# The start-up of a fused attention and feed-forward kernel: an order of work written out for all five engines

## The chip, the core and the metric

The kernel runs on one core of a Trainium2 chip. A core has five engines with a queue each, which work through their instructions in order and wait for one another by semaphores: TensorE (PE in the profile, with its weight loads as PEld), VectorE (DVE), ScalarE (ACT), GpSimd (POOL) and SyncE (SP), which here issues all transfers between the chip's memory and the core. The metric is the device time of one execution in microseconds; the median of three runs is given.

## The reference

Attention without a triangle: for 8 batches of 8 heads with 576 positions of 64 numbers, a softmax of each query over its 64 numbers, a softmax of the keys over the positions, one 64 x 64 matrix per head, and its product with the queries. The result is the input of a gated feed-forward layer of 4608 tokens:

```python
q_s = np.exp(q - np.max(q, axis=-1, keepdims=True))
q_s = q_s / (np.sum(q_s, axis=-1, keepdims=True) + 1e-09)
k_s = np.exp(k - np.max(k, axis=2, keepdims=True))
k_s = k_s / (np.sum(k_s, axis=2, keepdims=True) + 1e-09)
kv = np.einsum('bhsd,bhse->bhde', k_s, v)
attn = np.einsum('bhsd,bhde->bhse', q_s, kv)
x = attn.transpose(0, 2, 1, 3).reshape(4608, 512)
out = ((x @ w_a) * (x @ w_b)) @ w_out     # w_a, w_b: 512 x 1536; w_out: 1536 x 512
```

The three weight matrices arrive as 64-bit floating point numbers, the rest as 32-bit ones.

## The kernel before

The 4608 tokens are worked on in nine chunks of 512. For a chunk the attention makes `xf`, four tiles of 128 x 512 (one for each pair of heads); the feed-forward layer goes over d_ff in 12 blocks of 128 (`NF`, the index `f`).

*Chunk 0* is also where the weights are converted. For each half block, ACT makes two parts of the 64-bit numbers (L103, L104: `wy` and `wr`), DVE shifts (L107), GpSimd adds (L110), DVE joins them (L113), ACT rounds to the TensorE's short form (`ws`, a cast, L79 or L941), and DVE subtracts to get the rest (L82 or L946). The finished block goes to a DRAM copy (`dw`) that the later chunks read. With it TensorE does the gate of the block: 24 products of 128 x 512 (`pt`, L537), 12 for `w_a`, whose result ACT copies to `ga` (L544), and 12 for `w_b`, with which DVE multiplies `ga` (L548). `project_first` (`po`, L572) takes `ga` times the block of `w_out` in full 32-bit numbers, four products, each of two passes. In between stand the attention tasks of chunk 1, one with each block from f = 3 on: a key task has an exponential (`kv_exp_t`), transposes into `pka` and `pkb` with copies back to `kt` (L299 to L301) and a product `pk` (L314); a query task has a reduction, eight exponentials of `qt` (L385, L388), a multiply (L394), transposes into `pq` (L468) and a product `px`. A late key task has a maximum (`m`), a transpose `pm`, a reduction `mc` and a diagonal tile `m` (L263, L265), and a product `pmx` (L271).

*Chunks 1 to 8* use seven products in place of eight for the two gates of a pair of blocks (i = 0 to 5): `kx`, `ky`, `ka` and `kp` of 12 matmuls each (L562), on sums of x (`xo`, L503 to L526) and of weights (in chunk 1 made by GpSimd from `dy`, `ws_y`, and split by ACT and DVE). Their combination `cc` is split into `gh` and `gl`, and `project` (L583) multiplies these with the split `wo`. The tasks of the next chunk's attention are dealt out between the products by `attend`.

*What sets the order.* The program is traced in an order, and a scheduler that has a timing model of the engines decides each engine's final list within the dependences; `tc.issue_after(x)` keeps what it holds from going ahead of x, and a dependence of the class NoSync orders two instructions of one engine without a semaphore. Before the change, the first part of chunk 0 is a string of steps written by hand (L991 to L999: `mc0`, `qs0` ... `G2`, each a method of `Startup` and its numbers). `in_order` (L1010) then ties SP's instructions of that part into one chain, and likewise those of ACT, DVE and GpSimd; after the f loop it ties TensorE's from `by_hand` on. In the f loop the conversion of block f + 1 is held behind the end of gate f - 2 (L1035), the exponentials of a task behind the last step of the start and a gate's end (L1048), the first half's `ga` behind the copies of a task (L1060 to L1063). The rest is the scheduler's choice.

## Time and profile before

| | us |
|---|---|
| median of three runs | 964.56 (964.27 to 965.41) |
| profiled execution | 966.23 |
| its span | 964.4 |
| busy in the span: TensorE, DVE, ACT, GpSimd | 932.9, 624.6, 391.5, 105.5 |
| TensorE clock granted, mean over the span | 0.998 |

The slices of the page show where the engines are full:

```profile
PE   5899999899999999999999999999999999999998
DVE  7987878886686747665566657566666547553433
ACT  7787744452372416322443244223622263221111
```

Each of the 40 slices is 24.1 us, and a digit is the busy share in tenths, 9 being 90% or more. The first slice is the start, which waits for loads; chunk 0 goes on to about 150 us, so it fills the first six slices, and chunk 1 lies in the next four. The list of times an engine waited names what it wanted to write, then the engine, tile and line that it lacked; "longest" is the longest single wait. The time of a program part in the trace is from the start of the span.

### The profile page before, as it was taken

The page shows a single profiled execution, that of the slowest core. Times are in us where ns is not written, and L with a number is a line of the kernel's source. Part 1 is how long each engine was busy: PE and PEld are TensorE (multiplying, and loading weights), DVE is VectorE, ACT ScalarE, POOL GpSimd, SP SyncE. Part 2 cuts the span into 40 slices and gives each one's busy share as a digit, 9 for nine tenths or more (in the row PEclk, how much of TensorE's full clock was granted, in tenths as well). Part 3 has the DMA queues.
Part 4 walks back from the last instruction along what each step waited for, and adds up shares of the span by engine and source line. Part 5 has one row for each costly group of instructions (what it writes and reads, how often), then busy time and mean ns, then how long its engine had stood idle before and what let it go on. Part 6 is the DMA issues. An engine that isn't in the chain of part 4 may idle for free.

```text
span 964.4 us, 17587 instructions
## 1 busy us (share of the span) xinstructions
PE 932.9 (97%) x6479; PEld 828.2 (86%) x6479; DVE 624.6 (65%) x1209; ACT 391.5 (41%) x1085; POOL 105.5 (11%) x88
## 2 busy tenths in 40 slices
PE   5899999899999999999999999999999999999998
PEld 3656656889999999989999999999999999999997
DVE  7987878886686747665566657566666547553433
ACT  7787744452372416322443244223622263221111
POOL 1544342422000000000000000000000000000000
PEclk9999999999999999999999999999999999999999
DMA  9999686989998968897799779877987689667761
GB/s 348 412 381 390 214 274 214 407 276 332 323 357 297 359 238 273 305 368 256 258 330 356 268 244 351 316 280 258 344 304 286 240 289 305 243 236 266 258 211 56
DMA packets 97588, 282.64 MB, mean 293 GB/s; under 512 B 11680, under 2 KB 12256, under 8 KB 97504
## 3 DMA queue, kind: packets, MB, share of 16 engines
q1 hardware_dynamic: 97504, 281.52, 81.6%
q8 instruction: 52, 0.85, 0.3%
q14 instruction: 32, 0.26, 0.1%
HBM read 241.40 MB, written 37.98 MB: 290 GB/s over the span
## 4 chain that ended last, share of the span: by engine, by line
PE 79%; DVE 7%; DMA 5%; issue 4%; POOL 2%; ACT 2%; SPq 1%; DVEq 0%; POOLq 0%
PE po L583 27%; PE kp L562 13%; PE ka L562 13%; PE kx L562 13%; PE ky L562 7%; POOL wr L110 2%; PE px L493 2%; PE pk L314 2%; DMA ws<-dw 1%; DMA raw<-in_w_ab 1%; DVE wy L113 1%; PE pt L537 1%; DMA ws_y<-dy 1%; SPq L448 1%; DMA kt_first<-in_kt 1%
## 5 line engine op out<-in xcount | busy, mean ns | idle before, releaser
L583 PE MATMUL po<-wo_w,gh 128*128 128x512 f32 x768 | 226.3, 395 | 1.0 <-ACT gh L79 1.0
L562 PE MATMUL kx<-xo,ws 128*128 128x256 f32 x1152 | 162.7, 283 | 0.0
L583 PEld LDWEIGHTS po<-wo_w,gh 128*128 128x128 f32 x768 | 138.6, 188 | 27.6 <-ACT gh L79 1.5
L562 PE MATMUL ka<-xo,ws 128*128 128x256 f32 x1152 | 160.9, 282 | 0.4 <-DVE cc L1147 0.4
L562 PE MATMUL kp<-xo,ws 128*128 128x256 f32 x1152 | 157.6, 283 | 1.5 <-DVE u L1120 1.5
L562 PEld LDWEIGHTS ka<-xo,ws 128*128 128x128 f32 x1152 | 149.5, 188 | 4.7 <-DVE cc L1147 0.6
L562 PEld LDWEIGHTS kp<-xo,ws 128*128 128x128 f32 x1152 | 147.7, 188 | 5.2 <-issue 1.6
L562 PEld LDWEIGHTS kx<-xo,ws 128*128 128x128 f32 x1152 | 149.5, 188 | 2.5
L583 PE MATMUL po<-wo_w,gl 128*128 128x512 f32 x384 | 136.4, 396 | 0.0
L79 ACT CAST gh<-cc 128x512 fp32r<-128x512 f32 x96 | 56.6, 620 | 134.5 <-DVE cc L1144 128.2
L1143 DVE TENSOR_TENSOR cc<-kp,u 128x512 f32<-128x512 f32 x48 | 33.1, 689 | 99.1 <-PE kp L562 98.9
L1134 ACT COPY cc<-kx 128x256 f32<-128x256 f32 x48 | 17.8, 371 | 182.9 <-PE kx L562 182.8
L583 PEld LDWEIGHTS po<-wo_w,gl 128*128 128x128 f32 x384 | 71.2, 188 | 16.0 <-DVE gl L82 0.4
L407 ACT ACTIVATE qt<-qt,st 128x64 f32<-128x64 f32 x224 | 75.0, 339 | 22.4 <-DVE st L404 17.2
L1133 DVE TENSOR_TENSOR cc<-kp,u 128x512 f32<-128x512 f32 x48 | 33.1, 689 | 76.1 <-PE kp L562 75.9
L562 PE MATMUL ky<-xo,ws 128*128 128x256 f32 x576 | 77.6, 284 | 3.2 <-DMA ws<-dw 2.2
L562 PEld LDWEIGHTS ky<-xo,ws 128*128 128x128 f32 x576 | 71.9, 188 | 4.5 <-DVE gl L82 2.1
L82 DVE TENSOR_TENSOR gl<-cc,gh 128x512 fp32r<-128x512 f32 x96 | 64.6, 692 | 10.6 <-ACT gh L79 10.6
L537 PE MATMUL pt<-xo,ws 128*128 128x512 f32 x288 | 70.2, 399 | 1.1 <-DVE ws L946 1.1
L244 POOL PARTITION_ALL_REDUCE mx<-m x20 | 18.3, 915 | 446.5 <-DVE m L255 446.5
L537 PEld LDWEIGHTS pt<-xo,ws 128*128 128x128 f32 x288 | 53.5, 189 | 14.0 <-DVE ws L946 1.6
L1119 ACT COPY u<-kx 128x512 f32<-128x512 f32 x48 | 28.0, 584 | 84.6 <-PE kx L562 84.3
(147 smaller groups left out, 1155.6 us busy)
## 6 DMA issues: line engine op xcount, KB each, us to landing
ws<-dw SPq DMA_DIRECT2D x312, 512.0 KB, 5.5
dw<-ws SPq DMA_DIRECT2D x42, 512.0 KB, 7.2
mr<-dq SPq DMA_DIRECT2D x112, 128.0 KB, 4.6
raw<-in_w_ab SPq DMA_DIRECT2D x24, 512.0 KB, 8.0
out<-ot SPq DMA_DIRECT2D x36, 256.0 KB, 4.7
vt<-in_v SPq DMA_DIRECT2D x28, 325.0 KB, 6.9
qt<-in_q SPq DMA_DIRECT2D x32, 256.0 KB, 5.5
kt<-in_k SPq DMA_DIRECT2D x24, 320.0 KB, 5.1
```

Of the source, the lines that this page charges most:

```text
L79: nc.scalar.copy(out=hi, in_=src)
L82: return nc.vector.tensor_tensor(out=lo, in0=src, in1=hi.bitcast(F32), op=ALU.subtract)
L110: nc.gpsimd.tensor_tensor(out=r, in0=u, in1=r, op=ALU.add)
L314: nc.tensor.matmul(pk[h * D:(h + 1) * D], kt[:, j, h], vt[:, j, h], start=(j == 0), stop=(j == J - 1),)
L407: nc.scalar.activation(out=qt[:, j, h], in_=qt[:, j, h], func=AF.Exp, bias=st[:, h, 0, j:j + 1], accum_out=st[:, h, 1, j:j + 1],)
L493: nc.tensor.matmul(px[:, s], w, m[:, s], start=(i == 0), stop=(i == 2))
L537: nc.tensor.matmul(pt, w[:, wp], x[g][:, xp], start=(g == 0 and i == 0), stop=(g == NP - 1 and i == 2),)
L562: ins = nc.tensor.matmul(pt[:, n], w[:, n, wp, c], x[:, xp, c], start=(first and n == 0 and i == 0), stop=(i == 5), skip_group_check=True,)
L583: ins = nc.tensor.matmul(po[t], a[:, ts], wo[f][:, w], start=(f == 0 and i == 0), stop=(f == NF - 1 and i == 2),)
L1119: nc.scalar.copy(out=u2, in_=kx)
L1133: nc.vector.tensor_tensor(out=cc[:, 3], in0=kp, in1=u3, op=ALU.add)
L1143: nc.vector.tensor_tensor(out=cc[:, 1], in0=kp, in1=u2, op=ALU.add)
```

## The change

The scheduler's freedom in the first part of the program is replaced by a table. Each piece of the program from the first load to the start of chunk 2 gets a name: the steps of the start keep theirs, and in the f loop and in chunks 1 and 2 a context manager `named` notes the instructions that each engine receives under `gate.f`, `proj.f`, `out.f`, `a.f`, `b.f` (conversion of w_out and of the two halves), `soft.n`, `turn.n`, `prod.n` (a task's exponentials, transposes with copies, and product), `split.m`, `w<op>.n`, `pair.n`, `attend.n`, `x.1`, `raw.f`, `load.n`, `sums.n`. `ORDER` has a string of these names for each engine; `name*k` takes the next k instructions of a piece, `name:j` the one at place j of those still left. `arrange` puts the instructions into that order with NoSync dependences, and every later instruction of the engine behind the last of the list. The `issue_after` holds of the f loop and the `in_order` chains go, but for SP's first loads; in chunk 1 `attend` holds nothing back. The computation is the same, instruction for instruction.

```diff
+ORDER = {
+    "PE": (
+        "tr1*4 tr0*5 tr1 pk0*10 pk1*10 pq0*4 tr2*5 pq1*4 px0 tr3:4 tr3*4 pq2*4 pk2*10 pk3*10 px1 "
...
+    ),
+    "DVE": (
...
 
+    def named(name):
+        before = traced[-1]
+        yield
+        start = next(n for n in reversed(range(len(traced))) if traced[n] is before) + 1
+        for ins in traced[start:]:
+            work.setdefault((ins.engine, name), []).append(ins)
...
-        getattr(Startup, name)(*(int(n) for n in step[len(name):]))
+        with named(step):
+            getattr(Startup, name)(*(int(n) for n in step[len(name):]))
...
-    in_order((E.SP,), loads, by_hand)
-    in_order((E.Activation, E.DVE, E.Pool), by_hand, len(traced))
-    startup = [at["last", 0].ins, at["last", 1].ins]
+    def behind_each_other(instructions):
+        for ins, before in zip(instructions[1:], instructions):
+            tc.add_manual_dep(
+                ins, before.name,
+                mybir.DependencyInfo(mybir.DependencyClass.NoSync, mybir.DependencyReason.DATA),
+                reason="in order",
+            )
+    def arrange(engine, names):
+        left = {name: list(found) for (of, name), found in work.items() if of == engine}
+        chain = []
+        for item in names.split():
+            name, _, count = item.partition("*")
+            name, _, place = name.partition(":")
+            for _ in range(int(count or 1)):
+                chain.append(left[name].pop(int(place or 0)))
+        behind_each_other(chain)
+        placed = {ins.name for ins in chain}
+        for ins in traced[by_hand:]:
+            if ins.engine == engine and ins.name not in placed:
+                behind_each_other([chain[-1], ins])
+    behind_each_other([ins for ins in traced[loads:by_hand] if ins.engine == E.SP])
...
-        with tc.issue_after(at["end", f - 2].ins):
+        with named(f"out.{f}"):
             convert_wo(f)
...
-            with tc.issue_after(startup[0]), tc.issue_after(at["end", max(f - 2, 1)].ins):
+            with named(f"soft.{n + 1}"):
                 tasks[n + 1][1]()
...
-                    with ExitStack() as pinned:
-                        for copy in copies or ():
-                            pinned.enter_context(tc.issue_after(copy.ins))
                         at["ga", f] = gate_half(f, pts[0])
...
-    in_order((E.PE,), by_hand, len(traced))
...
+            def multiply(pt, op, xop, first):
+                w = operand(op)
+                with part("pair"):
+                    return product(pt, w, x[xop], first)
...
-                attend(last)
+                with part("attend"):
+                    attend(c > 1 and last)
...
+    for engine, names in ORDER.items():
+        arrange(getattr(E, engine), names)
```

What the table does is seen in the engines' lists. No engine has an instruction more or less. SP's list differs in one swapped pair (the load of a weight block and that of a query tile, late in chunk 1), GpSimd's in neighbours that change places, by three places at most. The lists of TensorE, DVE and ACT differ up to about 245 us of the old trace.

The first place is ACT's list ahead of the copy `kt_116<-pka_611`, the copy of the first key task's transposes. The names are tiles; a number tells two tiles of one name apart. `wy` and `wr` are the parts of a half block, `qt_569` and `qt_787` query tiles. Before:

```order
L79 CAST ws_590<-wy_583 128x2x256
L103 ACTIVATE wy_681<-wo4_raw_527 128x512
L104 ACTIVATE wr_682<-wo4_raw_527 128x512
L103 ACTIVATE wy_690<-raw_571 128x512
L104 ACTIVATE wr_691<-raw_571 128x512
L388 ACTIVATE qt_569,qst2_727<-qt_569,qst_725 128x64 x7
L79 CAST ws_604<-wy_597 128x2x256
L300 COPY kt_116<-pka_611 128x512
```

After it the copy stands in these rows:

```order
L416 ACTIVATE kt_116<-kt_116,mc_562 128x640
L226 ACTIVATE wy_583<-raw_523 128x512
L511 ACTIVATE qt_787,qst2_935<-qt_787,qst_933 128x64
L227 ACTIVATE wr_584<-raw_523 128x512
L423 COPY kt_116<-pka_611 128x512
L511 ACTIVATE qt_569,qst2_727<-qt_569,qst_725 128x64 x2
L511 ACTIVATE qt_787,qst2_935<-qt_787,qst_933 128x64
L667 COPY ga_520<-pt0_486 128x512
```

The copy has moved from row 74 to row 66 of ACT's list (like rows counted as one), ahead of the conversion of `wy_597`, `wo4_raw` and `raw_571`, and the exponentials, a block of seven before, are dealt out singly, those of two query tiles by turns.

The second place is TensorE's list around the same task: the transposes `pka_611` and `pkb_612` and the product `pk_652` that needs the copies. Before:

```order
L572 MATMUL po3_515<-yo1_370,ga_482 128x512
L299 MATMUL pka_611<-ident_66,kt_116 128x128 x4
L299 MATMUL pkb_612<-ident_66,kt_116 128x128
L537 MATMUL pt0_623<-xo_284,ws_543 128x512 x3
L537 MATMUL pt0_623<-xo_316,ws_543 128x512 x3
L537 MATMUL pt0_623<-xo_403,ws_555 128x512 x3
L537 MATMUL pt0_623<-xo_424,ws_555 128x512 x3
L537 MATMUL pt1_624<-xo_284,ws_543 128x512 x3
L537 MATMUL pt1_624<-xo_316,ws_543 128x512 x3
L537 MATMUL pt1_624<-xo_403,ws_555 128x512 x3
L537 MATMUL pt1_624<-xo_424,ws_555 128x512 x3
L314 MATMUL pk_652<-vt_118,kt_116 64x65 x10
```

After, with `pt0_486` and `pt1_487` the gate of f = 2 and `pt0_623` that of f = 3:

```order
L695 MATMUL po0_512<-yo1_370,ga_482 128x512
L660 MATMUL pt1_487<-xo_424,ws_474 128x512 x3
L422 MATMUL pkb_612<-ident_66,kt_116 128x128
L695 MATMUL po1_513<-yo1_370,ga_482 128x512
L695 MATMUL po2_514<-yo1_370,ga_482 128x512
L660 MATMUL pt0_623<-xo_284,ws_543 128x512 x3
L695 MATMUL po3_515<-yo1_370,ga_482 128x512
L660 MATMUL pt1_624<-xo_284,ws_543 128x512 x3
L695 MATMUL po3_515<-yo_529,ga_520 128x512
L422 MATMUL pka_716<-ident_66,kt_126 128x128 x4
L695 MATMUL po0_512<-yo_529,ga_520 128x512
L437 MATMUL pk_652<-vt_118,kt_116 64x65 x10
```

The four transposes into `pka_611` now stand three rows ahead of these, in the middle of the gate before. Between them and the product of their task are pieces of two gates and of two projections, and the next key task's transposes (`pka_716`) come ahead of that product.

The third place is DVE's list at the start of chunk 1. `xo` are the operands of chunk 1's products, `wo` the split output weights, `mc_1429` and `m1_1431` the reduction and the diagonal tile of the late key task. Before:

```order
L82 TENSOR_TENSOR xo_1398<-xt_1396,xo_1398 128x512
L521 TENSOR_TENSOR xt_1390<-xf_113,xt_1390 128x512
L82 TENSOR_TENSOR xo_1401<-xt_1389,xo_1401 128x512
L82 TENSOR_TENSOR wo9_w_1218<-wo9_w_1218 128x512
L263 TENSOR_REDUCE mc_1429<-pm_1427 128x1
L82 TENSOR_TENSOR xo_1404<-xf_113,xo_1404 128x512
L82 TENSOR_TENSOR xo_1407<-xf_113,xo_1407 128x512
L82 TENSOR_TENSOR xo_1411<-xt_1390,xo_1411 128x512
L265 TENSOR_SCALAR m1_1431<-ident_66,mc_1429 128x128
L82 TENSOR_TENSOR ws_1527<-ws_y_1439,ws_1527 128x2x256
```

After:

```order
L205 TENSOR_TENSOR ws_1322<-wy_1315,ws_1322 128x2x256
L634 TENSOR_TENSOR xt_1390<-xf_113,xt_1389 128x512
L386 TENSOR_REDUCE mc_1429<-pm_1427 128x1
L388 TENSOR_SCALAR m1_1431<-ident_66,mc_1429 128x128
L639 TENSOR_TENSOR xt_1396<-xf_113 128x512
L527 TENSOR_REDUCE st_1580<-qt_1581 128x2x4
L671 TENSOR_TENSOR ga_1367<-pt1_1354,ga_1367 128x512
L527 TENSOR_REDUCE st_1580<-qt_1643 128x2x4
L205 TENSOR_TENSOR xo_1393<-xt_1390,xo_1393 128x512
L205 TENSOR_TENSOR ws_1527<-ws_y_1439,ws_1527 128x2x256
```

The reduction and the diagonal tile stand next to each other, ahead of the splits of `xo_1393`, `xo_1398`, `xo_1401`, `xo_1404`, `xo_1407` and `xo_1411`; two reductions of the attention of chunk 2 (`st_1580`) have come in between, and the split of `wo9` has gone to a place much later in chunk 1.

## The prediction

> **What bounds the kernel now.** I read first where TensorE stands still, stage by stage, then what it waits for there, and last the engine that made it wait. The first view gives seven stretches of the span (964.4 us): bounds, length, then busy us and instructions of TensorE, its weight loads, DVE, ACT and POOL, the granted clock, the DMA share and GB/s:

> ```profile
> 0.00:26.90 26.90, 14.66 (x116) 10.46 (x116) 19.96 (x43) 21.51 (x60) 5.91 (x12) 1.00 0.94 354
> 26.90:60.00 33.10, 31.96 (x127) 22.29 (x124) 32.74 (x50) 24.44 (x48) 15.74 (x12) 1.00 1.02 403
> 60.00:70.00 10.00, 7.68 (x39) 3.87 (x38) 8.43 (x16) 9.15 (x25) 5.00 (x4) 0.83 0.99 365
> 70.00:150.00 80.00, 76.32 (x342) 51.54 (x341) 60.58 (x100) 51.97 (x125) 34.51 (x26) 1.00 0.78 284
> 150.00:200.00 50.00, 44.07 (x306) 36.77 (x305) 40.13 (x84) 27.38 (x95) 17.53 (x13) 1.00 0.88 329
> 200.00:300.00 100.00, 100.00 (x768) 92.94 (x767) 78.48 (x158) 43.83 (x125) 11.91 (x10) 1.00 0.94 326
> 300.00:964.40 664.40, 658.17 (x4794) 610.34 (x4793) 384.23 (x764) 213.20 (x611) 14.89 (x16) 1.00 0.78 277
> ```

> From 200 us on TensorE never rests for long: 100.00 of 100.00 us, then 658.17 of 664.40. Those 764 us are TensorE's own work, and the lists end there, so the change can give nothing in them. Everything it can win or lose lies in the first 200 us. There TensorE is idle 12.24 us before 26.9, and after that 33.10 − 31.96 = 1.14, 10.00 − 7.68 = 2.32, 80.00 − 76.32 = 3.68 and 50.00 − 44.07 = 5.93 us: **13.1 us** between 26.9 and 200.

> The second view lists TensorE's waits, by the tile it wanted to write and the tile it lacked (total, times, longest); the first fence is for 0 to 26.9 us, the second for 26.9 to 200, the third for all that follows:

> ```profile
> PE pka L846 <- ACT kt_first L840: 8.0, 2, 5.9
> PE pq L904 <- issue: 3.9, 2, 2.2
> ```
> ```profile
> PE pq L468 <- DVE qt L394: 2.2, 1, 2.2
> PE pmx L271 <- DVE m L265: 2.0, 1, 2.0
> PE pk L314 <- ACT kt L300: 1.9, 1, 1.9
> PE pka L299 <- ACT kt L293: 1.5, 1, 1.5
> PE kp L562 <- DVE u L1120: 1.5, 1, 1.5
> PE pt L537 <- DVE ws L946: 1.1, 1, 1.1
> PE po L583 <- ACT gh L79: 1.0, 1, 1.0
> ...
> ```
> ```profile
> PE ky L562 <- DMA ws<-dw: 2.2, 2, 2.0
> ...
> ```

> No entry of the middle list is a DMA, and each stands once. They are waits on a copy, an exponential or a subtraction of DVE or ACT that came late, while TensorE had other products ready behind it in its queue. That is what an order can mend.

> **The change part by part.** It adds and removes no instruction on any engine. All of its price is in who waits for whom. I take the edits by what they reorder.

> *Loads (SP).* SP's queue holds the same transfers in the same order but for one swapped pair. The loads land as before, so the first stage keeps its 12.24 us of idle time; its 8.0 us wait on the exponential of the keys hangs on those loads. Cost 0; from both sides I allow the 3.9 us of the pq row as a gain and the longest wait of that stage's pq, 2.2 us, as a loss.

> *GpSimd.* Its additions move by at most three places. Cost 0: it is busy 34.51 of 80.00 us, so its idle time hides such a swap; with that cover gone, one addition late is about one DVE operation stretched, priced under the rivals.

> *The wait at 60.7 us (pk on the copy of kt).* ACT's and TensorE's timelines (start, duration, instruction, idle before it):

> ```profile
> 59.22 0.34 ACT L388 ACTIVATE qt<-qt,qst 128x64 f32<-128x64 f32 x1
> ...
> 61.21 0.33 ACT L388 ACTIVATE qt<-qt,qst 128x64 f32<-128x64 f32 x1
> 61.54 0.60 ACT L79 CAST ws<-wy 128x512 fp32r<-128x512 f32 x1
> 62.05 0.57 ACT L300 COPY kt<-pka 128x512 f32<-128x512 f32 x1
> ```
> ```profile
> 62.67 0.80 PE L314 MATMUL pk<-vt,kt 128*64 128x65 f32 x20 [1.94 <-ACT kt L300]
> 63.41 5.40 PE L572 MATMUL po<-yo,ga 128*128 128x512 f32 x8
> ...
> 69.68 5.82 PE L537 MATMUL pt<-xo,ws 128*128 128x512 f32 x24
> ...
> 76.16 3.70 PE L572 MATMUL po<-yo,ga 128*128 128x512 f32 x8
> ```

> Seven exponentials and a cast, 59.22 to 62.05, stand ahead of the copy. In the new order they are spread out and the copy stands ahead of all but a few, and between the transposes and pk TensorE has pieces of two gates and two projections instead of one gate only. The 1.94 us go. What was hidden behind them is next: the same pieces of gate 4 and projection 2, whose operands are done by then.

> Behind that wait lies a second loss. The same eight passes of L572 take 5.40 us here and 3.70 us at 76.16, and the granted clock of that stretch shows why:

> ```profile
> 63.40:67.20 3.80, 3.80 (x9) 1.70 (x6) 3.73 (x8) 3.60 (x9) 1.27 (x1) 0.55 1.04 404
> ```

> After 1.94 us of idleness and twenty tiny products (pk, 0.80 us) the clock is 0.55 (the last but two of the columns). Without the wait I expect 1.00: **1.7 us** more (5.40 − 3.70). [...]

> *The waits of 70 to 150 us (pq on qt, pka on kt, pt on ws).* They have one answer: the exponentials and the multiply that feed a transpose now stand earlier in ACT's and DVE's lists, and TensorE's transposes stand later, cut in among a gate's triples. 3.68 us of idleness go. DVE is busy 60.58 of these 80.00 us, so it has 19.42 us in which to do the work earlier.

> *The waits of 150 to 200 us.* DVE's timeline before the pmx wait, which ends at 155.78:

> ```profile
> 149.96 1.78 DVE L82 TENSOR_TENSOR xo<-xt,xo 128x512 fp32r<-128x512 f32 x1
> 151.66 1.78 DVE L82 TENSOR_TENSOR wo_w<-wo_w 128x512 fp32r<-128x512 f32 x1
> 153.36 0.28 DVE L263 TENSOR_REDUCE mc<-pm 128x1 f32<-128x128 f32 x1
> 153.56 1.28 DVE L82 TENSOR_TENSOR xo<-xf,xo 128x512 fp32r<-128x512 f32 x2
> 154.76 0.68 DVE L82 TENSOR_TENSOR xo<-xt,xo 128x512 fp32r<-128x512 f32 x1
> 155.36 0.27 DVE L265 TENSOR_SCALAR m<-ident,mc 128x128 f32<-128x128 f32 x1
> ```

> Three splits stand between the reduction of mc and the product m, and two ahead of both. In the new order mc and m stand together ahead of them: that 2.04 us wait goes. But the splits that were passed are operands of chunk 1's first products (S1 with T1, A12 with B21, A22 with T4), and they are now later on a DVE that has 40.13 of 50.00 us filled. The rest of the stage's waits (kp on u, po on gh) are answers to a product just finished, and a filler must stand between. The new TensorE list puts pieces of projections there, but those pieces are single projections of 0.46 us a pass. I bound what stays by 0 and 5.93 us and take the middle, **3.0 us**.

> *The stretch 26.9 to 60.* DVE is busy 32.74 of 33.10 us, so a new order cannot make it shorter, only change who waits: two splits go out of it and two reductions come in, 0.67 to 0.68 us each. Its 1.14 us of idleness stay, with the break behind it.

> *Breaks.* Each wait also lets a matmul run out. The group line gives 399 ns for one matmul of L537, and 24 of them take 5.82 us (row at 69.68), so one starts every (5.82 − 0.40)/23 = 0.236 us:

> ```profile
> L537 PE MATMUL pt<-xo,ws 128*128 128x512 f32 x288 | 70.2, 399 | 1.1 <-DVE ws L946 1.1
> ```

> The views of idle time do not count the 0.16 us between; eleven waits (the four left out of the list are of 0.2 to 0.7 us) are **1.8 us**.

> **Sum.** 13.1 + 1.7 + 1.8 = 16.6 us can go. Of these 1.1 + 0.2 = 1.3 stay in the DVE-bound stretch and 3.0 at the start of chunk 1: gain 16.6 − 1.3 − 3.0 = **12.3 us**. The profiled execution took 966.23 us (span 964.4 and 1.8 around it), so it would take 953.9. The median of the runs before is 964.56, 1.67 lower; the same 12.3 us off it give **952.3 us**.

> **The rivals.**

> 1. *New waits take the place of half of the old.* The order is a list without slack: wherever ACT or DVE is 1 or 2 us later than the list supposes, TensorE stands, as it may not pass the piece. For it: the old list too had four waits of 1.5 to 2.2 us, and leads get shorter when TensorE comes earlier. Against it: between a piece and its user there is now work of more than one kind. Three new waits of 2.0 us (the longest rows above) cost 6.1: gain 6.2, 958.4 us. With a clock dip behind one or two of them only a quarter of the gain is left: 12.3/4 = 3.1, 961.5 us.

> 2. *Slower: the conversion of the weights becomes the bound.* Each half block goes ACT, DVE, POOL, DVE, ACT, DVE. The last split of the block of f = 5 and the gate that uses it stand so:

> ```profile
> 68.55 0.67 DVE L82 TENSOR_TENSOR ws<-wy,ws 128x512 fp32r<-128x512 f32 x1
> ```
> ```profile
> 80.05 5.83 PE L537 MATMUL pt<-xo,ws 128*128 128x512 f32 x24
> ```

> The split ends at 69.22 and the gate reaches its half block six products after 80.05, at 81.5: a lead of 12.2 us. TensorE will come there 2.3 + 1.7 + 0.5 = 4.5 us earlier (idleness, clock and breaks of the stretch from 60 to 70), and in the new list the split has 4.6 us more DVE work ahead of it: 3.1 us are left. A split that meets a GpSimd addition takes 1.78 in place of 0.68 us (rows at 151.66 and 154.76), 1.10 more; 26 GpSimd operations fall in 70 to 150 us, at worst 28.6 us against DVE's 19.42 us of idleness. [...] If each of gates 4 to 11 then waits w, the time is 952.3 + 8w; from w = 1.5 us it is no gain, and with w = 2.0, the size of the longest waits now, it is 968.3 us. Against it: those 19.42 us are there as they stand, with whatever meetings the old order had already in the 60.58, and the operations on GpSimd are the same.

> 3. *Nothing comes of it.* The pieces stand otherwise, but the waits only change names, as each chain is as long as before: 964.6 us.

> 4. *All goes, the start too.* Gain 16.6 + 3.9 (the pq row of the first stage) = 20.5: 944.1 us.

> **How the numbers follow.** Forecast, gain 8.5 to 16.6 us (948.0 to 956.1): 0.58. Rival 1, gain 1.9 to 8.5: 0.20. Rival 4 and what lies toward it: 0.07. Rival 3, within 0.2%, that is ±1.9 us, about what a measurement of this kernel can tell from no change: 0.06. Rival 2: 0.09. So faster 0.85, same 0.06, slower 0.09. The range goes from 944.0 (all goes) to 961.5 (a quarter is left); outside lie slower, same, and some 0.04 of the edges, about 0.2.

> **What would show it.** Right: in the new trace the middle list of waits sums to 4 or 5 us; pk no longer waits for the copy of kt, pmx not for m; no stretch near 63 us has a clock of 0.55; DVE's busy share between 60 and 150 us is higher; gate 3 still starts near its old time, and from the middle of chunk 1 on the two traces run at a constant distance of about 12 us. Wrong: new waits of gates on ws at 65 to 110 us (rival 2), waits of kp, ka or kx on xo or ws at the start of chunk 1 that sum to more than 3 us, a first stage that is longer than 26.9 us, or L572 passes that cost more where they stand between a gate's triples.

## The result, and the profile after

The changed kernel takes 949.58 us (median of 5 runs, 947.33 to 951.55), the kernel before 964.56 (5 runs, 963.07 to 965.41): a ratio of 0.9843, 95% interval 0.9826 to 0.986, or 15.1 us less (13.5 to 16.8). The forecast was 952.3 us, 12.3 less. The profiled execution took 951.55 us, span 949.7, the slowest of the five; 14.7 less than the profiled one before. One profile among the experiments fell in an execution with a granted clock of 0.753; it is not read here, and another was taken.

The stretches of the new profile, with the columns of the old ones (TensorE, weight loads, DVE, ACT, GpSimd, clock, DMA share, GB/s):

```profile
0.00:26.90 26.90, 14.94 (x127) 11.60 (x128) 19.30 (x49) 21.16 (x59) 5.41 (x11) 1.00 0.95 351
26.90:60.00 33.10, 33.10 (x143) 22.52 (x142) 27.60 (x48) 30.96 (x79) 17.73 (x12) 1.00 1.03 412
60.00:70.00 10.00, 10.00 (x60) 7.32 (x59) 7.76 (x16) 6.61 (x12) 4.58 (x3) 1.00 0.98 354
70.00:150.00 80.00, 79.26 (x356) 54.22 (x355) 67.08 (x113) 56.95 (x141) 36.62 (x27) 1.00 0.92 338
150.00:200.00 50.00, 48.42 (x356) 42.33 (x355) 39.51 (x90) 22.33 (x71) 16.89 (x12) 1.00 0.87 315
200.00:300.00 100.00, 98.31 (x762) 90.35 (x761) 74.70 (x151) 40.61 (x119) 8.63 (x8) 1.00 0.95 328
300.00:949.70 649.70, 644.33 (x4686) 597.60 (x4684) 377.71 (x749) 211.87 (x608) 14.90 (x16) 1.00 0.78 278
```

Between 26.9 and 200 us TensorE now idles 0.00 + 0.00 + 0.74 + 1.58 = 2.3 us, where it was 13.1. From 200 to 300 it idles 1.69 us, where it was 0.00. Its waits of 26.9 to 200 us, and then those of all that follows:

```profile
PE kx L685 <- DMA ws<-dw: 1.3, 1, 1.3
PE ky L685 <- DVE ga L671: 0.7, 1, 0.7
PE pm L384 <- DVE m L378: 0.3, 1, 0.3
```
```profile
PE ka L685 <- DVE cc L1313: 1.1, 1, 1.1
PE ky L685 <- DMA ws<-dw: 0.8, 1, 0.8
PE ky L685 <- DVE xf L802: 0.7, 2, 0.4
PE po L706 <- ACT gh L202: 0.6, 1, 0.6
```

All seven waits of 1 us or more that the old list had there are gone, the one of chunk 0's gates on `ws` among them (another wait of po on gh, 0.6 us, has come at 250 us). The longest that is left, 1.3 us, is on a transfer, which the old list did not have there. And the gates start sooner; the first product of a gate in the new and in the old timeline:

```profile
23.93 2.03 PE L660 MATMUL pt<-xo,ws 128*128 128x512 f32 x6
```
```profile
26.91 1.42 PE L537 MATMUL pt<-xo,ws 128*128 128x512 f32 x5
```

To compare stages of runs that do their work in different orders, I use TensorE's **loss**: the time that has gone by, less the start-to-start times of the matmuls started by then. These are read from unbroken rows: 232 ns for `pt` and for `project`, 119 for the products of 256 columns, 429 for a pass of `project_first`, 109 for a transpose of 128 columns, 39 for a product of `pk`. In every run here they sum to about 916 us; a stage is good to about half a microsecond. By stage, in the two profiled executions:

| stretch, us | loss before | loss after |
|---|---|---|
| 0 to 40 | 18.9 | 16.1 |
| 40 to 60 | 1.5 | 0.4 |
| 60 to 70 | 4.3 | 0.2 |
| 70 to 150 | 5.3 | 1.9 |
| 150 to 200 | 7.8 | 2.3 |
| 200 to 320 | 1.2 | 4.1 |
| 320 to 930 | 4.9 | 3.9 |

So 2.7 us come from the start, about 14 from 40 to 200 us, and 2.9 are given back in 200 to 320. This last figure is of one pair of executions: the other profiles that have the old order there lose 1.7 to 3.0 us, those with the new one 2.9 to 3.3, so about 1 us is given back as a rule. Behind 320 us, where the lists do not differ, the profiles lose between 2 and 6.5 us.

### The profile page after: what moved, and what is told of

The parts are those of the page before. It is cut to its first block, busy times and chain, and to the rows that moved or that the text cites. A ratio compares the mean times of both kernels' runs of the same rounds, so it can differ in the third digit from the quotient of the medians.

```text
span 949.7 us, 17529 instructions
## 1 busy us (share of the span) xinstructions
PE 928.4 (98%) x6479; PEld 825.9 (87%) x6479; DVE 613.7 (65%) x1209; ACT 390.5 (41%) x1085; POOL 104.8 (11%) x88
## 4 chain that ended last, share of the span: by engine, by line
PE 89%; DMA 4%; DVE 4%; SPq 1%; ACT 1%; issue 1%; DVEq 0%; ACTq 0%
PE po L706 27%; PE kp L685 13%; PE ka L685 13%; PE kx L685 13%; PE pt L660 7%; PE ky L685 7%; PE po L695 4%; PE px L616 2%; PE pk L437 2%; DMA ws<-dw 1%; DMA mr<-dq 1%; SPq L571 1%; DMA raw<-in_w_ab 1%; PE px L604 1%; DVE ws L205 1%
## 5 line engine op out<-in xcount | busy, mean ns | idle before, releaser
L660 PE MATMUL pt<-xo,ws 128*128 128x512 f32 x288 | 86.7, 441 | 0.0
L530 ACT ACTIVATE qt<-qt,st 128x64 f32<-128x64 f32 x224 | 75.2, 340 | 21.3 <-DVE st L527 18.2
```

Of the source, the lines that this page charges most:

```text
L530: nc.scalar.activation(out=qt[:, j, h], in_=qt[:, j, h], func=AF.Exp, bias=st[:, h, 0, j:j + 1], accum_out=st[:, h, 1, j:j + 1],)
L660: nc.tensor.matmul(pt, w[:, wp], x[g][:, xp], start=(g == 0 and i == 0), stop=(g == NP - 1 and i == 2),)
```

## The experiments

All are the new program text with another table; "old order" and "new order" are the two programs' lists up to the start of chunk 2. A ratio is to the kernel before, run beside it.

**1. Is it the order?** `old_table` holds the old lists, so that each engine has the old order to the last instruction.

```diff
     "PE": (
-        "tr1*4 tr0*5 tr1 pk0*10 pk1*10 pq0*4 tr2*5 pq1*4 px0 tr3:4 tr3*4 pq2*4 pk2*10 pk3*10 px1 "
+        "tr0*5 tr1*5 pk0*10 pk1*10 pq0*4 pq1*4 tr2*5 px0 tr3*5 px1 pk2*10 pq2*4 pk3*10 g00*12 pq3*4 "
...
```

> The new program text with the table filled with the old order, for all five engines up to the start of chunk 2; behind that the rest follows as before. Theory (only the order counts): the time of the kernel before, 964.6 us, within 2 us. Rival (the way the order is held, by a chain of dependences in place of holds on instructions, counts too): off by more than 2 us on either side.

Ratio 1.0005 (0.9988 to 1.0022), median 965.61 against 966.18. The order makes the difference, not the way in which it is held. And this profile, of the same order, differs from the old one in a telling place. Its TensorE timeline around 63 us:

```profile
63.38 0.80 PE L444 MATMUL pk<-vt,kt 128*64 128x65 f32 x20 [1.95 <-ACT kt L430]
64.11 3.70 PE L702 MATMUL po<-yo,ga 128*128 128x512 f32 x8
67.64 0.60 PE L429 MATMUL pka<-ident,kt 128*128 128x128 f32 x4
70.31 0.30 PE L429 MATMUL pkb<-ident,kt 128*128 128x128 f32 x1 [2.07 <-DVE wholes L455]
```

The wait of pk is there, 1.95 us, but no low clock: the eight passes take 3.70 us, not 5.40. Nothing is won by it, since pkb now waits 2.07 us for DVE's `wholes` where in the profile before it waited 0.38:

```profile
69.62 0.30 PE L299 MATMUL pkb<-ident,kt 128*128 128x128 f32 x1 [0.38 <-DVE wholes L325]
```

The 1.7 us of low clock and the growth of pkb's wait, 1.69 us, are the same time. That gave a second theory, called B below (the forecast's reading, each wait a loss of its own, is A): DVE's and ACT's lists set the time at which gate 4 may start, and what TensorE does before only decides where it stands.

**2. New order up to a point.** The pieces that stand ahead of the point in the old lists are put in the new order, the rest in the old. Three points: the first product of gate 2, of gate 4, and of chunk 1. The lines of TensorE's list in which the points lie, in that order:

```diff
+        "g10*3 g01:6 g01:6 g01:6 g01*3 g11:6 g11:6 g11:6 g11:6 g11:6 g11:6 g01*6 g11*6 g20*12 g21*12 "
...
+        "turn.1 gate.4*24 prod.1*10 proj.3*4 turn.2*4 gate.5*24 prod.2*2 proj.4*4 turn.3*5 gate.6*24 "
...
+        "gate.11:3 gate.11:3 gate.11*3 pair.0*12 prod.8 proj.10*4 pair.0*12 proj.0 pair.0*12 proj.0*3 "
```

> New order for what stands ahead of the first product of gate 2 (40.6 us in the old trace), old order behind it. Theory (the start was shortened, which the forecast put at nothing): TensorE's loss up to 40 us is 18.85 us in the old trace and 16.1 in the new, so 2.7 us less, 961.9 us. Rival (the filled DVE of 40 to 60 us takes it back, as the forecast had it): 964.6 us.

Ratio 0.9979 (0.9963 to 0.9996), 2.0 us less (0.4 to 3.6). The start did get shorter: loss up to 40 us is 16.5 here, and in the seven profiles with the new start it is 15.7 to 16.6, in the six that have the old start 18.9 to 20.7. TensorE comes 2.5 us sooner to the wait of pt on ws (at 40.14 us, before at 42.65) and loses 0.7 of it there (1.8 us of wait, 1.1 before). The rest is kept: gate 4 starts at 67.88 us, before at 69.68. Here the low clock is back behind the same wait:

```profile
60.88 1.06 PE L446 MATMUL pk<-vt,kt 128*64 128x65 f32 x20 [1.94 <-ACT kt L432]
61.87 5.08 PE L704 MATMUL po<-yo,ga 128*128 128x512 f32 x8
```

> New order up to the first product of gate 4 (69.7 us in the old trace), old order behind it. Theory (the wait of pk on kt, the low clock and the waits of 40 to 60 us go here): loss up to 70 us is 24.6 us in the old trace, 16.6 in the new, so 8.0 us less, 956.6 us, and no stretch near 60 us with a clock of 0.55. Rival (TensorE meets weights that are not ready, as the conversion in the old order has leads of 7.7 us and more only because TensorE is late): new waits of pt on ws, half of it left, 960.6 us.

Ratio 0.9995 (0.9983 to 1.0007): nothing. Up to 60 us TensorE is 4.2 us ahead of the old run, up to 70 us 5.1, and between 70 and 110 it loses 8.3 us, where the old run lost 2.3. Not on weights, as the rival had it, but on the attention tasks, and behind each of these two waits the clock is 0.50 for 3.4 us, which is 1.7 us more each time (waits of 20 to 320 us):

```profile
PE pka L433 <- ACT kt L427: 4.0, 1, 4.0
PE pk L448 <- ACT kt L434: 3.9, 1, 3.9
...
```

One of the two is the seam's own: the casts of w_out that the new order puts off past the point stand there in a heap, four in 2.17 us, just ahead of the copy that pk waits for:

```profile
67.58 2.17 ACT L213 CAST wo_w<-yo 128x512 fp32r<-128x512 f32 x4
69.66 0.66 ACT L238 ACTIVATE wr<-wo_raw 128x512 int32<-128x512 uint32 x1
70.22 0.56 ACT L434 COPY kt<-pka 128x512 f32<-128x512 f32 x1
```

> New order up to the first product of chunk 1 (152.2 us in the old trace), old order behind it. Theory (each stage's waits go by its own order): loss up to 150 us is 29.9 us in the old trace, 18.7 in the new, so 11.2 us less, 953.4 us; the waits kp on u, ky on cc, po on gh of chunk 1 stand as before. Rival (chunk 1's order has nothing to do with its waits, and they only follow from DVE being behind): the time of the new order, 949.6 us.

Ratio 0.99 (0.9884 to 0.9917), 9.7 us less, 956.27: between the old order and the new. Taken off 964.56, that is 954.9 us (953.4 to 956.6), so the theory's 953.4 is at the edge and the rival's 949.6 is out. Loss from 40 to 110 us is 1.0 as in the new order. Here too a heap stands at the seam (ky waits 3.7 us at chunk 1's start, and the clock is 0.50 for 3.4 us behind it), and kp on u is back with 1.5 us.

**3. Chunk 1 alone.** `new_from_chunk1`: the old order up to the first product of chunk 1, the new one behind it.

```diff
     "PE": (
-        "tr1*4 tr0*5 tr1 pk0*10 pk1*10 pq0*4 tr2*5 pq1*4 px0 tr3:4 tr3*4 pq2*4 pk2*10 pk3*10 px1 "
+        "tr0*5 tr1*5 pk0*10 pk1*10 pq0*4 pq1*4 tr2*5 px0 tr3*5 px1 pk2*10 pq2*4 pk3*10 g00*12 pq3*4 "
...
+        "proj.9*4 turn.8 gate.11*24 prod.8 proj.10:2 proj.10:1 pair.0*24 proj.10 proj.0 pair.0:24 "
```

> Old order up to the first product of chunk 1, new order behind it. Theory (the order of chunk 1 is worth what its stage lost less: 7.8 us of loss in 150 to 200 us before, 2.3 after, but 1.2 before and 4.1 after in 200 to 320): 2.6 us less, 962.0 us. Rival (chunk 1's part needs what the new order puts off and draws ahead in chunk 0): no gain, 964.6 us.

Both wrong: ratio 1.0052 (1.0032 to 1.0072), 5.0 us **more**. Loss in 150 to 320 us is 15.5 us, where the old order had 9.0 and the new one has 6.4. The wait of pmx, 2.0 us before, has grown, and others are new; behind the first two of these rows the clock is 0.50 for 3.4 us:

```profile
PE pmx L402 <- DVE kvh L212: 3.2, 1, 3.2
...
PE ky L693 <- DVE ga L679: 1.9, 1, 1.9
...
PE px L624 <- ACT qh L210: 0.9, 1, 0.9
```

The same chunk 1 behind a new chunk 0 is worth 956.27 − 949.58 = 6.7 us (5.5 to 6.4 by the ratios of 0.99, 0.9843 and 0.9834); behind the old chunk 0 it costs 5.0. The parts do not add. Neither figure is the price of chunk 1's order alone: each has a seam, and most of the 6.7 us can be that of `new_to_chunk1`, 3.7 us of wait and 1.7 of low clock. By 40 us this profile had also lost about 1.8 us more than the old one, with the clock at 0.50 from 27.3 to 30.7 us, where the lists are the old ones.

**4. One copy.** `copy_first` is the old order with ACT's copy of `pka_611` drawn ahead of the exponentials.

```diff
-out.4*2 a.5*2 soft.2*7 b.4 turn.0 b.5*2 soft.2
+out.4*2 a.5*2 turn.0 soft.2*7 b.4 b.5*2 soft.2
```

> Old order with one instruction moved: ACT's copy of the first key task's transposes (kt_116) stands ahead of the eight exponentials of qt, not behind seven of them. Theory A (the forecast's: the wait of pk and the low clock behind it are losses of their own): both go, 3.6 us less, 961.0 us. Theory B (DVE's chain bounds 55 to 70 us; in the run with the old order in the table the same wait of 1.95 us came without a low clock, and the wait of pkb on wholes grew from 0.38 to 2.07 us instead): pk's wait goes, pkb's grows by as much, gate 4 starts as late as before, 964.6 us within 1 us.

Theory B holds: ratio 0.9994 (0.9978 to 1.0011). pk no longer waits and no low clock follows it; pkb waits for all of it, 0.38 + 1.94 + 1.7 = 4.0 us:

```profile
61.22 0.80 PE L444 MATMUL pk<-vt,kt 128*64 128x65 f32 x20
61.95 3.70 PE L702 MATMUL po<-yo,ga 128*128 128x512 f32 x8
65.49 0.60 PE L429 MATMUL pka<-ident,kt 128*128 128x128 f32 x4
70.16 0.30 PE L429 MATMUL pkb<-ident,kt 128*128 128x128 f32 x1 [4.07 <-DVE wholes L455]
70.22 7.37 PE L667 MATMUL pt<-xo,ws 128*128 128x512 f32 x24
```

The low clock has moved with the wait: it is 0.50 from 70.4 to 73.8 us, and gate 4 takes 7.37 us in place of 5.82. That is not lost either, as the next wait, pka on kt, is 0.2 us in place of 1.5.

**5. The copy and the scaling.** In `copy_first` pkb waits 4.07 us until DVE has scaled the product before it, whose tag `at` it has in the kernel. `copy_scale_first` draws DVE's three scaling instructions ahead too.

```diff
-out.4 b.4 a.5 b.5
+out.4 b.4 prod.0*3 a.5 b.5
...
-gate.3 prod.0 a.5 out.5 prod.0 b.5 prod.0
+gate.3 a.5 out.5 b.5
```

> Old order with ACT's copy of kt_116 ahead of the exponentials, as in copy_first, and with DVE's three instructions that scale pk_652 into wholes (den, reciprocal, wholes) right behind the subtraction of ws_604 instead of eight to twelve places later. Theory B (the pair of lists bounds, DVE's place for the scaling decides when pkb may be written): the 4.1 us wait of pkb that copy_first shows goes, gate 4 starts at about 66 us instead of 70. If the stretch behind it is TensorE's, 4 us less, 962 us. Theory C (from gate 4 to 110 us ACT and DVE bound too, as the run with the new order up to gate 4 gave back 8 us there): gate 4 starts 4 us earlier, but the waits pka on kt and pq on qt grow by the 4 us, 966 us.

> The kernel of copy_scale_first for one more profile, as the one of its own run was of an execution with a granted clock of 0.753. Theory C: pkb does not wait, gate 4 starts at about 66 us; behind it pka on kt and pq on qt and others wait for more than the 3.7 us that they do in the old trace, by 4 us or more, up to 110 us; TensorE's loss up to 110 us is as in the old trace (27 us) or higher.

Theory C, and worse than its 966 us: ratio 1.0034 (1.0019 to 1.0048), 3.3 us more; the execution with the second profile took 966.05 us beside 965.73, one run of each. The second profile shows gate 4 at 66.17 us, 3.5 us sooner than before, and then a wait of pka on the next key task's exponential:

```profile
66.17 5.85 PE L667 MATMUL pt<-xo,ws 128*128 128x512 f32 x24
...
92.65 0.89 PE L429 MATMUL pka<-ident,kt 128*128 128x128 f32 x4 [4.99 <-ACT kt L423]
```

In the profile before:

```profile
91.75 0.66 PE L299 MATMUL pka<-ident,kt 128*128 128x128 f32 x4 [1.47 <-ACT kt L293]
```

TensorE reached the same place 2.6 us sooner and left it 0.9 later. Behind this wait of 5 us the clock is 0.50 for 3.4 us, and the next gate takes 7.15 us in place of 5.83; loss up to 110 us is 29.4, before 27.0. That exponential, in ACT's timelines of this run, of the kernel before and of the new order:

```profile
91.77 0.83 ACT L423 ACTIVATE kt<-kt,mc 128x640 f32<-128x640 f32 x1 [1.22 <-DVE mc L422]
```
```profile
90.87 0.83 ACT L293 ACTIVATE kt<-kt,mc 128x640 f32<-128x640 f32 x1 [1.22 <-DVE mc L292]
```
```profile
76.88 0.83 ACT L416 ACTIVATE kt<-kt,mc 128x640 f32<-128x640 f32 x1 [0.24 <-DVE mc L415]
```

It does not move with TensorE: in the old order it stands, with the reduction `mc` of DVE that it waits for, behind conversions of weights that are early. From gate 5 on DVE's splits end 11 to 17 us ahead of their first use. In the new order it comes 14 us sooner. No run moves this exponential by itself.

**6. Only the putting-off.** `old_wo_late`: the old order with the splits of w_out where the new one has them (here DVE's first two).

```diff
-a.3 b.3 split.2 out.3 a.4
+a.3 b.3 out.3 a.4
...
-a.3 b.3 split.3 a.4 b.4
+a.3 b.3 a.4 b.4
...
+gate.4 a.6 split.2 soft.4 prod.1
...
+attend.1:13 split.3 pair.1
```

> Old order with one theme of the change: the twelve pairs of split instructions of w_out (a cast on ACT, a subtraction on DVE), which nothing needs before chunk 1, stand where the new order has them, each behind its neighbour there. Theory B (ACT and DVE, with the conversion of weights, bound 27 to 70 us): two splits less there give ACT 1.2 and DVE 1.4 us, gate 4 starts 1 to 2 us earlier; 1.5 to 4 us less in all, about 962 us. Theory A (each wait is for a single late copy): pk's wait shrinks by the two casts, 1.2 us, nothing else, 963.4 us. Rival (the splits only collide with chunk 1's work instead): 965 us or more.

All three wrong in sign or place (the rival has the sign, but the loss lies ahead of chunk 1): ratio 1.0051 (1.0033 to 1.0069), 4.9 us more. pk's wait shrank to 0.7 us as theory A had it, but pkb waits 2.0, and later the two waits on attention pieces grow from 2.2 and 1.5 us:

```profile
PE pq L598 <- DVE qt L524: 3.8, 1, 3.8
PE pka L429 <- ACT kt L423: 2.7, 1, 2.7
```

The place where a split is put takes time from what stands behind it there. The two waits are 2.8 us longer together, and behind each the clock is 0.50 for 3.4 us, 1.7 us more each time. What part of the 4.9 us this is stays open: the start of this profile, where the lists are the old ones, lost 1.8 us more than before too, with the clock at 0.50 from 27.9 to 31.3 us.

**7. How much slack is left?** In the old order the split of gate 5's second half ends at 69.22 and is used at 81.5. In the new one DVE's row and TensorE's are:

```profile
74.24 0.68 DVE L205 TENSOR_TENSOR ws<-wy,ws 128x512 fp32r<-128x512 f32 x1
```
```profile
75.24 1.96 PE L660 MATMUL pt<-xo,ws 128*128 128x512 f32 x6
```

The lead is 75.24 − 74.92 = 0.3 us in place of 12.3. `late_split` puts this one subtraction seven places later (the text on record counts eight).

```diff
-b.6 a.6 b.5 out.6 a.7 prod.1*2 soft.4 soft.3 out.6 a.6 split.2
+b.6 a.6 out.6 a.7 prod.1*2 soft.4 soft.3 out.6 b.5 a.6 split.2
```

> New order with one instruction moved: DVE's subtraction for the second half block of gate 5 (ws_709) stands eight instructions later, behind the join of wy_889, about 4 us. In the new trace it ends 0.3 us ahead of its use (74.9 and 75.2 us), in the old one 12.3. Theory B (in the new order TensorE and the conversion of weights reach gates 3 to 6 together, with no slack): TensorE waits about 3.5 us there and the time is 953 us. Rival (the conversion has slack that later work gives back): less than 1.5 us, 951 us or less.

953.4 us (ratio 0.9865, 0.9844 to 0.9886): 3.8 more than the 949.58 and 3.4 more than the 950.01 of the new order in its second measurement; by the ratios, each to the kernel before beside it, 2.1 and 3.0 more, with intervals that touch. The wait on `ws` is there:

```profile
79.08 2.08 PE L685 MATMUL pt<-xo,ws 128*128 128x512 f32 x4 [2.70 <-DVE ws L230]
```

The wait is 2.7 us, and behind it the clock is 0.50 for 3.4 us, 1.7 us more: together the 4.5 us that the stage 70 to 110 us lost more than in the new order. Of these some 3 are still lost at 320 us. The theory's 953 us came out, but not by its sum: the expected 3.5 us of wait were 0.8 too many, and the low clock was not in it.

**8. Two waits that are left.** `two_moves_in_new` moves two DVE instructions of the new order, `new_again` is the new order beside it.

```diff
-w3.0 attend.1:2 w5.0 gate.11 split.0
+w3.0 attend.1:2 gate.11 w5.0 split.0
...
-w5.4 attend.2 pair.3:3 pair.3:3 pair.3*2 pair.3:1
+w5.4 pair.3:3 pair.3:3 pair.3*2 attend.2 pair.3:1
```

> New order with two DVE instructions moved: the product that ends gate 11 (ga_1465) ahead of a split of a weight sum, as ky waits 0.74 us for its bank, and the subtraction of kt_1835 behind four combinations of cc, as ka waits 1.08 us for the first of them. Theory (each of these waits is for one instruction in front of its releaser): both go, 1.8 us less than the new order run beside it. Rival (the waits move to the next product): the same as the new order.

> The new order as it is, beside the others on the same chip: 0.984 of the time before.

Ratios 0.9848 (0.983 to 0.9866) and 0.9834 (0.9813 to 0.9854): the same. The two waits are absent from the profile of the one, but also from that of the other, which is the new order itself; `new_again` has these in place of them:

```profile
PE kx L685 <- DMA ws<-dw: 1.4, 1, 1.4
PE px L616 <- DVE ql L205: 0.7, 1, 0.7
PE pm L384 <- DVE m L378: 0.6, 1, 0.6
...
```

Waits of under about 1 us in this part change from execution to execution. No version here beats the new order.

One engine's new list with the others' old ones was not tried, so how the gain is divided among the engines' lists stays open.

## Why the prediction was right, and where its steps were off

**Where the gain would come from** was right: the waits between 26.9 and 200 us, by an order that lets ACT and DVE finish in time. The forecast's 12.3 us and the measured 15.1 differ by two terms that it had set too low, the start (2.7 us more) and the stretch to 60 us (1.1 more); the other three came to 0.4 to 1.0 us less than forecast each, and 1.0 us of the two profiles' difference lies behind 320 us, where executions differ by more than that. So the sum is closer than its terms, in part because they err both ways.

- *The start, put at 0* ("the loads land as before, so the first stage keeps its 12.24 us"). Its idle time stayed, 11.96 us in 26.9, but the gates' first products were drawn into it ahead of the last transposes and products of the start; gate 0 begins 3.0 us sooner. Loss up to 40 us fell by 2.7, and `new_to_gate2`, which has the new start, is 2.0 us faster (0.4 to 3.6) though it gives 0.7 back behind pt on ws. This is the largest mis-sized term. Of the signs named ahead, the one that gate 3 would start near its old time failed with it: it starts at 49.87 us, before at 54.92.
- *"DVE is busy 32.74 of 33.10 us, so a new order cannot make it shorter"*, 1.3 us kept. It did: DVE is busy 27.60 us of the same stretch, and TensorE never idle. What looked full was in part stretched. The splits there, before and after:

```profile
L946 DVE TENSOR_TENSOR ws<-wy,ws 128x512 fp32r<-128x512 f32 x5 | 6.5, 1329 | 0.2 <-ACT ws L941 0.2
L82 DVE TENSOR_TENSOR ws<-wy,ws 128x512 fp32r<-128x512 f32 x3 | 3.2, 1102 | 0.0
```
```profile
L1069 DVE TENSOR_TENSOR ws<-wy,ws 128x512 fp32r<-128x512 f32 x4 | 3.8, 960 | 0.2
L205 DVE TENSOR_TENSOR ws<-wy,ws 128x512 fp32r<-128x512 f32 x4 | 3.7, 914 | 0.9 <-ACT ws L202 0.9
```

  By the forecast's own rows such a split is 0.68 us when GpSimd is not at work. The old profile bears this out: its splits of 128x512 take 0.67 to 0.69 us where no GpSimd operation runs at the same time, and up to 1.81 us where one does. An order moves these meetings too. Eight splits take 2.2 us less here (9.7 to 7.5) and eight joins of `wy` 1.0 less (7.5 to 6.5); about 1.5 of the 5.1 us are other work standing there. No run tries this by itself.
- *The stretch 60 to 70, 4.5 us.* The loss fell by 4.1, so the sum was right; the reasons were not, and the agreement is luck. The forecast added 1.9 us of wait and **1.7 us of low clock** as separate losses that go with one copy. `old_table` has the wait without the low clock, `copy_first` neither of them at pk, and both take the time of before: the next wait, on DVE's scaling, filled what was won. That the low clock came of the lull fits: of the four profiles with this wait of 1.94 or 1.95 us (before, `new_to_gate2`, `new_from_chunk1`, `old_table`) three have it. But at this place it was not a loss of its own.
- *70 to 150, 4.2 us.* Loss 5.3 to 1.9: 3.4. The reason given, pieces that stand earlier on a DVE with 19 us of idle time, is a part of it. `copy_scale_first` points to another: in the old order ACT's exponential for the next key task came at 91 us, however soon TensorE was there. So the gain seems to need the attention pieces to pass weights that were wanted 12 us later, as the new order has them; this is read from the rows, not shown by a run of its own.
- *Chunk 1, half of 5.93 us kept.* Loss in 150 to 200 fell by 5.5 us, but 2.9 of it came back between 200 and 320: 2.6 net, where the forecast's was 5.93 − 3.0 and the breaks. Over the other profiles of the two orders the net is 2 to 5 us. The amount was right; the place of what stays was not: the waits named (kp on u, po on gh) went while others came.

**The rivals.** Rival 2 had the mechanism of the gain and took it for a danger: the leads of the weights do fall, from 12.3 to 0.3 us at gate 5 (the rival had 3.1), and that is what the new order pays with. It stops just short; `late_split` puts a price on seven places more, 2 to 4 us. Rival 1 is what happens to the half measures: `new_to_gate4`, `copy_first` and `copy_scale_first` remove waits and get them back, in part as low clock.

## What to carry to other kernels

A list of waits is not a list of savings: take one away in the profile, ask which engine's list sets the next one, and follow it until the time has somewhere to go. When several in-order engines feed one another, look for work that is early by much (a lead of 12 us) standing ahead of work that is late; exchanging them has to be done on all lists together, and a part of the exchange may cost more than it brings. An engine that is full in a stage may be full of operations that another engine stretches, as DVE was in the old profile of splits that take 0.67 to 0.69 us alone and up to 1.81 beside GpSimd's work; compare their mean with that of the same form elsewhere before calling it a bound.

## What the runs showed of the hardware

A lull does not always bring the low clock. The same order, with the same wait of 1.94 or 1.95 us and the same twenty small products, was followed by eight passes of 5.40 us (before), 5.08 us (`new_to_gate2`) and 3.70 us (`old_table`).

A stretch at 0.50 cost up to 1.7 us (eight passes took 5.40 us in place of 3.70). Behind pk the kernel's time did not show it: pkb waits 0.38 and 0.44 us behind the two low clocks, and 2.07 behind the full one. Over whole executions it does not look free: of 64 of the kernel before, the 22 with a mean clock of 0.998 or more took 965.1 us in the mean, the 41 with 0.996 or less 966.7. In ten of the new order the mean clock was 0.998 to 1.0, so a part of the gain can be time at the full clock.
